# Windowed attention with a max-out layer on one core: weight sums in the third feed-forward bank, fillers in the transpositions' bank, weights loaded behind a group's second part

## The chip, the core and the metric

The kernel runs on one core of one Trainium2 chip. A core has TensorE (PE in the profile, with its weight loads as PEld), VectorE (DVE), ScalarE (ACT), GpSimd (POOL) and SyncE (SP, which here only issues transfers). Each takes its instructions in the order in which they stand in its own queue, and waits at the head of that queue for what an instruction needs. The metric is device time in microseconds, the median of several runs.

## The reference

Attention over 8 batches, 8 heads, 576 positions and 64 values a head, in a window of 128 positions with a bias that falls with distance; then a layer that takes the largest of three products, and one more product:

```python
scores = scale * np.matmul(q, k.transpose(0, 1, 3, 2))
bias = slopes[:, None, None] * (-np.abs(rel).astype(np.float32))[None, :, :]
mask = (rel >= 0) & (rel < window)
scores = np.where(mask, scores + bias[None], -1000000000.0)
attn = np.exp(scores - np.max(scores, axis=-1, keepdims=True))
attn = attn / (np.sum(attn, axis=-1, keepdims=True) + 1e-09)
attn_out = np.matmul(attn, v)
x = attn_out.transpose(0, 2, 1, 3).reshape(B * S, H * D)      # 4608 x 512
h = np.maximum(np.maximum(x @ w1, x @ w2), x @ w3)            # 4608 x 768
out = h @ w_out                                               # 4608 x 512
```

## The kernel before

**Attention.** A task is one batch and one pair of heads: 8 batches make 32 tasks, four to a batch. A task has five steps, one for each block of 128 query rows (the last has 64). For a step, `products` makes the scores on PE (into ps_s, or into ps_m0 and ps_m1), `score` folds the window and adds the bias on DVE (L323, L326, L338), `exps` takes exponentials on ACT (L352), `sums_of` and `normalise` divide by their sums (L360, L361, L373 on ACT or L368 on POOL), `turn` transposes two steps at a time on PE into the bank pt (L382) and ACT copies them out (L386, L392, L395), POOL cuts them to the window (L396, L400), and `mix` multiplies by v on PE into ps_x (L422). After a task's last step ACT copies the mixed values to SBUF (L431).

**Feed-forward.** A batch's x is split in seven combinations of its quarters (`factors_x`, L448 and L449, after DVE differences at L452), each in a high and a low part. A `unit` is one of seven products (L573) of a group; there are eleven groups a batch, nine for the three first matrices and two for the last.

**Weights.** The matrices come as 12 groups of 1 MB. For each, `preparing` takes six steps: `exponents` and `convert` repack the raw words (L144, L145, or L147, L148; then L154 or L158, and L161), and four calls of `part`. Parts 0 and 1 cut the raw words in high and low (`hi_lo`: L167 on ACT, L168 on DVE). Parts 2 and 3 add and subtract them on PE by products with an identity (`plus`) and its negative (`minus`): L178, into a tile of PSUM, which `hi_lo` empties. After part 3 the group is stored (keep, L205) for the later batches. The raw words of a group live in one of two buffers, hs2; `fetch` (L130) loads them through SP's queue. They are last read in part 1.

**Fillers.** `spin` issues products of zeros by zeros on PE (L263) that nobody reads, seven at the start and two at each of 24 steps, into one tile in the bank ps_m2. That bank is the third of the three that the units take in turn (ps_m0, ps_m1, ps_m2), and no unit uses it in the prologue. The transpositions and the weight sums share the bank pt. All these tiles have one buffer each: whoever takes the bank next waits until the one before is read.

**Order.** The prologue is the first batch's attention, with weight steps between (1.3 for each attention step from step 3 on); there is no feed-forward work yet except the first units. From then on a batch's feed-forward runs beside the next batch's attention. Calls are listed with a due time (`at`) and sorted; in the first two batches a scheduler then orders the instructions of each engine by its own estimate, taking the listed order as priority, so that the final queues differ from the code's order. `fix` ends that for PE.

The names in the rows below end in a buffer's number: the same number is the same tile.

Of the kernel before, what the change touches and what calls it, by code (L numbers as in the profile page):

```python
# [8 lines left out]
F32 = mybir.dt.float32  # L9
# [11 lines left out]
LAG_T, LAG_X = 4, 6  # L21
# [1 line left out]
SHIFT = (0, 2, 4)  # L23
O_PACE = 0.285
RING = 2
SPIN, FIRST_SPIN = 2, 7


FEW = 4
# [3 lines left out]
def attention_maxout_kernel(  # L33
# [12 lines left out]
    P = 128  # L46
# [4 lines left out]
    NG = w_all.shape[0]  # L51
    W = 2 * P
# [17 lines left out]
    ps_m = ctx.enter_context(tc.tile_pool(name="ps_m", bufs=1, space=PSUM))  # L70
    ps_s = ctx.enter_context(tc.tile_pool(name="ps_s", bufs=1, space=PSUM))
    ps_t = ctx.enter_context(tc.tile_pool(name="ps_t", bufs=1, space=PSUM))
# [27 lines left out]
    def slopes(hp):  # L100
        for h in (2 * hp, 2 * hp + 1):
            nc.scalar.activation(bias[:, h, :], dist, AF.Copy, scale=-8.0 * 2.0 ** (-8.0 * (h + 1) / H))
        nc.gpsimd.affine_select(
            out=bias0[:, 2 * hp:2 * hp + 2], in_=bias[:, 2 * hp:2 * hp + 2], pattern=[[0, 2], [-1, P]],
            compare_op=ALU.is_ge, fill=-NEG, base=0, channel_multiplier=1,
        )
# [21 lines left out]
    def fetch(g):  # L128
        r = raws[g] = hs_p.tile([P, 4 * DM + DM // 2], I32, name="hs2", bufs=2)
        nc.sync.dma_start(r.bitcast(U8)[:, :16 * DM - 3], w_all[g].bitcast(U8)[:, 3:])  # L130
# [7 lines left out]
    def words(g, j):  # L138
        return pieces(g)[0][:, j * DM:(j + 1) * DM].bitcast(F32)

    def exponents(g, few):
        _, t, top, small = pieces(g)
        if few:
            nc.vector.tensor_scalar(out=small, in0=top, scalar1=-56.0, scalar2=56.0, op0=ALU.max, op1=ALU.min)  # L144
            nc.scalar.activation(t.bitcast(F32), top, AF.Copy, scale=2.0 ** 27)  # L145
        else:
            nc.scalar.activation(small, top, AF.Relu, bias=-56.0)  # L147
            nc.scalar.activation(t.bitcast(F32), top, AF.Relu, scale=-2.0 ** 27, bias=-56.0 * 2.0 ** 27)  # L148

    def convert(g, few):  # L150
        u, t, _, small = pieces(g)
        u = u.bitcast(U32)
        if few:
            nc.vector.scalar_tensor_tensor(  # L154
                out=t, in0=small, scalar=-2.0 ** 27, in1=t.bitcast(F32), op0=ALU.mult, op1=ALU.add
            )
        else:
            nc.vector.scalar_tensor_tensor(  # L158
                out=t, in0=small, scalar=2.0 ** 27, in1=t.bitcast(F32), op0=ALU.mult, op1=ALU.subtract
            )  # L160
        nc.vector.scalar_tensor_tensor(  # L161
            out=u, in0=u, scalar=5, in1=t.bitcast(U32), op0=ALU.logical_shift_right, op1=ALU.bitwise_or
        )

    def hi_lo(t, src):
        pick = (lambda a: t[:, :, a]) if len(t.shape) == 4 else (lambda a: t[:, a])
        nc.scalar.copy(out=pick(0), in_=src)  # L167
        nc.vector.tensor_tensor(out=pick(1), in0=src, in1=pick(0).bitcast(F32), op=ALU.subtract)  # L168

    def group(g):  # L170

        if g < 9:
            return lambda a, e, d=1: wts[g, a // 4][:, a - a // 4 * 4:e - a // 4 * 4:d]
        return lambda a, e, d=1: ow[:, a:e:d, g - 9]

    def added(t, *terms):
        for n, (sign, x) in enumerate([(sign, x[:, a]) for sign, x in terms for a in (1, 0)]):
            nc.tensor.matmul(  # L178
                t, lhsT=sign, rhs=x, start=n == 0, stop=n == 2 * len(terms) - 1, skip_group_check=True,
            )  # L180

    def part(g, n):
        if g < 9 and n == 0:
            place(g, 0)
        if g < 9 and n == 1:
            place(g, 1)
        f = group(g)
        one = lambda k: f(k, k + 1)[:, 0]
        if n < 2:
            src = words(g, n).rearrange("p (k n) -> p k n", k=2)  # L190
            hi_lo(f(0, 2) if n == 0 else f(4, 7, 2), src)
            return
        ps = ps_t.tile([P, 2, W], F32, name="pt")
        if n == 2:
            added(ps[:, 0], (plus, one(1)), (plus, one(6)))
            added(ps[:, 1], (plus, one(0)), (minus, one(1)))
            hi_lo(one(1), ps[:, 0])
            hi_lo(one(5), ps[:, 1])
        else:
            added(ps[:, 0], (plus, one(1)), (minus, one(0)))  # L200
            added(ps[:, 1], (plus, one(4)), (minus, one(1)), (plus, one(0)))
            hi_lo(f(2, 4), ps)
            if g < 9:
                for a in range(2):
                    nc.sync.dma_start(keep[g][a], wts[g, a].bitcast(F32))  # L205

    def place(n, a):
        wts[n, a] = wt_p.tile([P, 4 - a, 2, W], F32R, name=f"wt{a}")

    def ahead(n, a):  # L210

        return n < RING or (n - RING, 6 if a else 3) in used


    g_order = [0, 1, 9, 10, 11, 2, 3, 4, 5, 6, 7, 8]

    def preparing():
        for n, g in enumerate(g_order):
            exponents(g, n < FEW)
            yield  # L220
            convert(g, n < FEW)
            yield
            for k in range(4):
                while g < 9 and not ahead(g, k > 0):
                    yield True
                part(g, k)
                yield
            if n + 2 < NG:
                fetch(g_order[n + 2])

    prepared, owed = 0, 0
    steps_of_weights = preparing()

    def weights(n=0, upto=0):
# [21 lines left out]

    idle = hs_p.tile([P, P + 512], mybir.dt.bfloat16, name="hs")
    nc.vector.memset(idle, 0.0)
    spun = ps_m.tile([P, 512], F32, name="ps_m2")

    def spin(n):
        for _ in range(n):
            tc.keep_in_program_order(nc.tensor.matmul(  # L263
                spun, lhsT=idle[:, :P], rhs=idle[:, P:], start=True, stop=True, skip_group_check=True,
            ))

    fixed = False

    def pe(ins):
        if fixed:  # L270
# [7 lines left out]
    def load(t):  # L278
        b, hp = tasks[t]
        qkt[t] = qk_p.tile([P, 2, S], F32, name="qk")  # L280
        for cs in (slice(0, 2 * P), slice(2 * P, S)) if t == 0 else (slice(0, S),):
            nc.sync.dma_start(qkt[t][:, :, cs], qk[b, hp, :, :, cs])

    def load_v(t):
        b, hp = tasks[t]
        vt[t] = v_p.tile([P, NB, P], F32, name="v")
        nc.sync.dma_start(vt[t], v[b, hp])
# [152 lines left out]
    def later(when, what, *args):  # L440
        todo.append((when, what, args))
        todo.sort(key=lambda x: x[0])
# [3 lines left out]
    def split(out, src, e):  # L446
        hi, lo = out
        nc.scalar.copy(out=hi, in_=src)  # L448
        e.tensor_tensor(out=lo, in0=src, in1=hi.bitcast(F32), op=ALU.subtract)  # L449

    def sub(out, x, y):
        nc.vector.tensor_tensor(out=out, in0=x, in1=y, op=ALU.subtract)  # L452

    def factors_x(b, when, step):
        t0, t1 = [xk[b, k][:, :, :C] for k in range(2)], [xk[b, k][:, :, C:] for k in range(2)]
        b00, b01, b10, b11 = t0[0], t1[0], t0[1], t1[1]
        new = {}

        def tmp():
            new["t"] = xk_p.tile([P, 2, C], F32, name="xt")  # L460
            return new["t"]

        def cut(k, src):
            xs[b, k] = x = xs_p.tile([P, 2, 2, C], F32R, name="xs")
            split((x[:, 0], x[:, 1]), src(), nc.vector)

        t = lambda: new["t"]
        for n, (k, diff, src) in enumerate((
            (0, None, lambda: b00),
            (1, lambda: sub(tmp(), b01, b00), t),  # L470
            (2, lambda: sub(t(), b11, t()), t),
            (3, lambda: sub(b01, b11, b01), lambda: b11),
            (4, None, lambda: b10),
            (5, None, lambda: b01),
            (6, lambda: sub(b10, b10, t()), lambda: b10),
        )):
            if diff:
                later(when + n * step, diff)
            later(when + n * step, cut, k, src)
# [111 lines left out]
    def at(when, what, *args):  # L591
        events.append((when, len(events), what, args))

    n_steps = NP * NB
    shift = [SHIFT[min(b, 2)] for b in range(B)]
    for t, (b, hp) in enumerate(tasks):
        for i in range(NB):
            s = t * NB + i + shift[b]
# [32 lines left out]
            when += pace if u < 77 * b + 63 else O_PACE  # L631
    for u in range(77 * B, 77 * B + 3):
        at(when, unit, u)
    for s in range(3, n_steps + LAG_X):
        at(s + 0.2, weights, 1.3)
    for s in range(n_steps + LAG_X - 2):
        at(s + 0.45, spin, SPIN)

    def fix():
# [2 lines left out]

    at(2 * n_steps + LAG_X + shift[2], fix)
    spin(FIRST_SPIN)
    load(0)
    nc.sync.dma_start(ident, c_ident)
    nc.scalar.copy(out=plus, in_=ident)
    nc.scalar.activation(minus, ident, AF.Copy, scale=-1.0)
    slopes(0)
    fetch(0)  # L650
    load_v(0)
    load(1)
    fetch(1)
    for _, _, what, args in sorted(events, key=lambda e: e[:2]):
# [39 lines left out]
```

## Time and profile before

| what | value |
|---|---|
| median of 3 runs | 819.0 us (817.31 to 820.26) |
| profiled execution | 814.65 us, span 812.9 us |
| mean granted TensorE clock | 0.993 |
| TensorE, VectorE, ScalarE, GpSimd busy | 783.2, 551.0, 536.1, 192.7 us |
| fillers (L263) | 55 products, from 2.5 to 77.2 us |
| first and fourth copy of mixed values (L431) | 36.17 and 79.45 us |
| loads of raw weights (L130) | 12, issued from 2.8 to 142.8 us, median 5.5 us to landing |

A row of a timeline has the start, the length, the engine, the line, the operation, the tile written and those read, their shapes, how many instructions are merged, and in brackets how long the engine stood idle before and what ended that. A matmul of 32-bit numbers can show as two records. A list of waits names who waited for whom: total, times and the longest. The clock is a share of full speed.

### The profile page before, as it was taken

Reading aid. Unit: us, or ns where it says so; the run is one execution under the profiler, and the core shown is the slowest. Engines: PE = TensorE matmul, PEld = TensorE weight load, DVE = VectorE, ACT = ScalarE, POOL = GpSimd, SP = SyncE. Lnnn points to the kernel's source line nnn. Section 1 sums busy time; section 2 is a strip of 40 time slices with the busy share of each in tenths; the row PEclk is TensorE's granted clock in tenths of the full one; section 3 lists DMA queues with packets and bytes.
Section 4 is the critical chain, followed back from the end, with each engine's and each line's share of the span. In section 5 each row is a group of like instructions: output and inputs, shape, how many; then the busy total and the mean of one; then the engine's idle time right before and its main releaser. Section 6 shows DMA issues by size and latency. Waiting matters only on the chain.

```text
span 812.9 us, 18197 instructions
## 1 busy us (share of the span) xinstructions
PE 783.2 (96%) x6543; PEld 687.8 (85%) x6543; DVE 551.0 (68%) x1771; ACT 536.1 (66%) x1796; POOL 192.7 (24%) x412
## 2 busy tenths in 40 slices
PE   7887999999999999999999999999999999999997
PEld 2445877789898999899988998899898989899897
DVE  4776888977577937776567846785667847673662
ACT  5688788677676866676667756775667757652342
POOL 2332213212232212231232212321222213211100
PEclk8999999999999999999999999999999999999999
DMA  6663368585788648873698558873797557765851
GB/s 230 235 225 133 122 247 307 189 288 188 237 276 278 239 134 287 299 257 139 212 313 275 199 173 284 302 258 113 243 318 248 192 199 252 258 214 176 291 204 59
DMA packets 41674, 184.81 MB, mean 227 GB/s; under 512 B 4592, under 2 KB 13552, under 8 KB 32368
## 3 DMA queue, kind: packets, MB, share of 16 engines
q0 software_dynamic: 18144, 115.61, 42.4%
q1 hardware_dynamic: 23296, 67.97, 23.3%
q8 instruction: 52, 0.85, 0.4%
q14 instruction: 38, 0.31, 0.1%
q10 hardware_dynamic: 144, 0.07, 0.0%
HBM read 157.68 MB, written 25.95 MB: 226 GB/s over the span
## 4 chain that ended last, share of the span: by engine, by line
PE 76%; issue 7%; DVE 6%; ACT 5%; DMA 4%; POOL 1%; SPq 0%; POOLq 0%; ACTq 0%; DVEq 0%
PE ps_m L573 54%; PE ps_x L422 8%; PE ps_s L308 6%; PE pt L382 5%; DMA hs<-in_w_all 3%; PE pt L178 2%; ACT p L352 1%; DVE hs L449 1%; DMA wt<-keep 1%; POOL wt L254 1%; DVE s L338 1%; ACT hs L147 1%; DVE t L536 1%; DVE hq L537 1%; DVE ps_s L326 1%
## 5 line engine op out<-in xcount | busy, mean ns | idle before, releaser
L573 PE MATMUL ps_m<-xs,wt 128*128 128x288 f32 x3024 | 430.9, 298 | 7.3 <-DVE xs L449 2.8
L573 PEld LDWEIGHTS ps_m<-xs,wt 128*128 128x128 f32 x3024 | 407.4, 188 | 15.7 <-DVE hq L531 3.0
L582 ACT COPY t<-ps_m 128x288 f32<-128x288 f32 x264 | 104.2, 395 | 73.9 <-PE ps_m L573 72.8
L573 PE MATMUL ps_m<-hs,ow 128*128 128x288 f32 x1008 | 140.5, 296 | 1.2 <-DVE hs L449 0.7
L573 PEld LDWEIGHTS ps_m<-hs,ow 128*128 128x128 f32 x1008 | 134.4, 188 | 3.3 <-DVE hs L449 2.3
L396 POOL TENSOR_SCALAR_AFFINE_SELECT pp<-pr 128x256 f32<-128x256 f32 (+1 forms) x128 | 60.3, 471 | 322.7 <-ACT pr L395 189.7
L352 ACT ACTIVATE p<-s,st 128x128 f32<-128x128 f32 (+1 forms) x320 | 127.4, 402 | 8.5 <-PE pt L382 3.3
L254 POOL DMA_DIRECT2D wt<-keep x126 | 67.8, 538 | 207.3 <-PE ps_m L573 199.4
L373 ACT ACTIVATE p<-p,st 128x128 f32<-128x128 f32 x280 | 97.4, 397 | 17.8 <-DVE st L361 17.8
L536 DVE TENSOR_TENSOR t<-ps_m,t 128x288 f32<-128x288 f32 x144 | 64.5, 452 | 47.3 <-PE ps_m L573 30.4
L338 DVE CUSTOM_DVE_ANT_0 s<-ps_s,bias 128x128 f32<-128x128 f32 (+1 forms) x300 | 76.9, 283 | 18.5 <-PE ps_s L308 13.9
L326 DVE COPY_PREDICATED ps_s<-prev,ps_s 128x256 f32<-128x256 uint8 x120 | 50.8, 423 | 48.4 <-PE ps_s L308 46.6
L422 PE MATMUL ps_x<-pp,v 128*64 128x256 f32 (+3 forms) x768 | 79.9, 322 | 0.6 <-POOL pp L396 0.5
L308 PE MATMUL ps_s<-qk 64*64 64x192 f32 (+1 forms) x1080 | 70.5, 328 | 3.2 <-DVE st L338 3.2
L537 DVE TENSOR_TENSOR hq<-t,hq 128x288 f32<-128x288 f32 x144 | 66.6, 466 | 2.4
L422 PEld LDWEIGHTS ps_x<-pp,v 128*64 128x64 f32 (+1 forms) x768 | 45.8, 136 | 26.5 <-issue 10.7
L395 ACT COPY pr<-pt 128x256 f32<-128x256 f32 x64 | 18.9, 321 | 71.0 <-PE pt L382 71.0
L382 PE MATMUL pt<-ident,p 128*128 128x128 f32 (+1 forms) x320 | 56.9, 286 | 7.9 <-DVE wt L168 3.6
L382 PEld LDWEIGHTS pt<-ident,p 128*128 128x128 f32 (+1 forms) x320 | 33.8, 141 | 34.6 <-issue 18.5
L352 ACT ACTIVATION_READ_ACCUMULATOR p<-s,st 128x1 f32 (+1 forms) x320 | 62.0, 194 | 0.0
L308 PEld LDWEIGHTS ps_s<-qk 64*64 64x64 f32 x1080 | 40.8, 134 | 21.8 <-issue 8.8
L400 POOL TENSOR_SCALAR_AFFINE_SELECT pp<-pr 128x256 f32<-128x256 f32 (+1 forms) x128 | 56.5, 441 | 0.0
(71 smaller groups left out, 760.4 us busy)
## 6 DMA issues: line engine op xcount, KB each, us to landing
wt<-keep POOLq DMA_DIRECT2D x63, 1024.0 KB, 7.5
wt<-keep POOLq DMA_DIRECT2D x63, 768.0 KB, 4.9
qk<-in_qk SPq DMA_DIRECT2D x31, 576.0 KB, 5.8
hs<-in_w_all SPq DMA_DIRECT2D x12, 1023.6 KB, 5.5
v<-in_v SPq DMA_DIRECT2D x32, 320.0 KB, 5.8
keep<-wt SPq DMA_DIRECT2D x9, 1024.0 KB, 5.5
outT<-t SPq DMA_DIRECT2D x64, 144.0 KB, 1.8
keep<-wt SPq DMA_DIRECT2D x9, 768.0 KB, 3.7
```

The source lines that it names most:

```text
L254: nc.gpsimd.dma_start(wts[n, a], keep[n % 9][a])
L308: pe(nc.tensor.matmul(ps[j][d:d + D, o:o + k1 - k0], lhsT=qkt[t][j * D:(j + 1) * D, 0, q0:q0 + D], rhs=qkt[t][j * D:(j + 1) * D, 1, k0:k1] ...
L338: nc.vector.tensor_tensor_reduce(out=s[:n], in0=ps[j][:n, P:2 * P], in1=(bias if i else bias0)[:n, 2 * hp + j, :], scale=-0.125, scalar=3. ...
L352: nc.scalar.activation(p[:n, j], s[:n], AF.Exp, bias=st[:n, 0, a, j:j + 1], scale=-1.0, accum_out=st[:n, 1, a, j:j + 1])
L373: nc.scalar.activation(p[:n, j], p[:n, j], AF.Copy, scale=st[:n, 2, a, j:j + 1])
L382: pe(nc.tensor.transpose(out=pt[:, a, j, :n], in_=p[:n, j], identity=ident[:n, :n]))
L396: nc.gpsimd.affine_select(out=pp[t, i - 1][:, :, 1, :n], in_=r[:, a, :, :n], pattern=[[0, 2], [-1, n]], compare_op=ALU.is_gt, fill=0.0, ba ...
L422: pe(nc.tensor.matmul(x[j * D:(j + 1) * D, c:c + e - a], lhsT=vv[:n, i, j * D:(j + 1) * D], rhs=w[:n, j].rearrange("p a b -> p (a b)")[:, ...
L536: nc.vector.tensor_tensor(out=s, in0=ps, in1=e, op=ALU.add)
L537: nc.vector.tensor_tensor(out=h, in0=s, in1=h, op=ALU.max)
L573: pe(nc.tensor.matmul(ps, lhsT=lt, rhs=rt, start=i == 0 and k in (0, 1, 4), stop=i == len(pairs) - 1, skip_group_check=True,))
L582: nc.scalar.copy(out=e, in_=ps)
```

## The change

Six edits, all in what the prologue does:

- The tile of parts 2 and 3 (L193) is in the bank ps_m2 as long as the first batch's x has not been cut (`begun`), and in pt afterwards.
- `spin` takes a new tile in pt at each call, where it had one in ps_m2.
- Fillers come four at every second step, where they were two at each.
- A group's successor but one is fetched after its part 1, where it was after its part 3.
- Weight steps begin at step 5 with 1.5 for each attention step, where they began at 3 with 1.3.
- At the start the first v is loaded ahead of the identity, and the first bias is made ahead of `plus` and `minus`.

```diff
-SPIN, FIRST_SPIN = 2, 7
+SPIN, FIRST_SPIN = 4, 7
...
-        ps = ps_t.tile([P, 2, W], F32, name="pt")
+        ps = ps_t.tile([P, 2, W], F32, name="pt") if begun else ps_m.tile([P, 2, W], F32, name="ps_m2")
...
                 part(g, k)
+                if k == 1 and n + 2 < NG:
+                    fetch(g_order[n + 2])
                 yield
-            if n + 2 < NG:
-                fetch(g_order[n + 2])
...
-    spun = ps_m.tile([P, 512], F32, name="ps_m2")
 
     def spin(n):
+        spun = ps_t.tile([P, 512], F32, name="pt")
         for _ in range(n):
...
-    fixed = False
+    fixed = begun = False
...
     def factors_x(b, when, step):
+        nonlocal begun
+        begun = True
...
-    for s in range(3, n_steps + LAG_X):
-        at(s + 0.2, weights, 1.3)
-    for s in range(n_steps + LAG_X - 2):
+    for s in range(5, n_steps + LAG_X):
+        at(s + 0.2, weights, 1.5)
+    for s in range(1, n_steps + LAG_X - 2, 2):
         at(s + 0.45, spin, SPIN)
...
     load(0)
+    load_v(0)
     nc.sync.dma_start(ident, c_ident)
+    slopes(0)
+    fetch(0)
     nc.scalar.copy(out=plus, in_=ident)
     nc.scalar.activation(minus, ident, AF.Copy, scale=-1.0)
-    slopes(0)
-    fetch(0)
-    load_v(0)
```

What the scheduler makes of it is seen in the queues. First DVE at the start of the program. Before, the instruction behind the three memsets is the first on the raw weights (hs2_160), ahead of the first scores (s_177 and s_179 are the two heads of step 0):

```order
L258 MEMSET hs_139 128x320
L144 TENSOR_SCALAR hs2_160<-hs2_160 128x1024
L338 ISA s_177,st_176<-ps_s_105,bias0_117 128x128
L338 ISA st_176 128x1
L338 ISA s_179,st_176<-ps_s_105,bias0_117 128x128
```

Now, from the second head of step 0 on:

```order
L338 ISA s_179,st_176<-ps_s_105,bias0_117 128x128
L338 ISA st_176 128x1
L323 COPY_PREDICATED ps_m0_199<-prev_113,ps_m0_199 128x128
L326 COPY_PREDICATED ps_s_105<-prev_113,ps_s_105 128x2x128
L323 COPY_PREDICATED ps_m1_200<-prev_113,ps_m1_200 128x128
L338 ISA s_187,st_176<-ps_s_105,bias_116 128x128
L338 ISA st_176 128x1
L338 ISA s_189,st_176<-ps_s_105,bias_116 128x128
L338 ISA st_176 128x1
L338 ISA s_212,st_211<-ps_m0_199,bias_116 128x128
L338 ISA st_211 128x1
L144 TENSOR_SCALAR hs2_160<-hs2_160 128x1024
```

Five scores stand ahead of L144.

Second, DVE at the last step of the second task (s_427 and s_429 are its two heads). Before, with the second group's raw words hs2_166 and the third's hs2_409:

```order
L338 ISA s_427,st_426<-ps_s_105,bias_116 64x128
L338 ISA st_426 64x1
L154 SCALAR_TENSOR_TENSOR hs2_166<-hs2_166 128x1024
L168 TENSOR_TENSOR wt1_328<-pt_331,wt1_328 128x256
L161 SCALAR_TENSOR_TENSOR hs2_166<-hs2_166 128x1024
L144 TENSOR_SCALAR hs2_409<-hs2_409 128x1024
L168 TENSOR_TENSOR wt0_435<-hs2_166,wt0_435 128x2x256
L168 TENSOR_TENSOR wt0_288<-pt_358,wt0_288 128x2x256
L168 TENSOR_TENSOR wt1_486<-hs2_166,wt1_486 128x2x256
L154 SCALAR_TENSOR_TENSOR hs2_409<-hs2_409 128x1024
L338 ISA s_429,st_426<-ps_s_105,bias_116 64x128
```

Now (s_480 and s_482 are the next task's first step):

```order
L154 SCALAR_TENSOR_TENSOR hs2_166<-hs2_166 128x1024
L168 TENSOR_TENSOR wt0_328<-ps_m2_387,wt0_328 128x256
L338 ISA s_427,st_426<-ps_s_105,bias_116 64x128
L338 ISA st_426 64x1
L338 ISA s_429,st_426<-ps_s_105,bias_116 64x128
L338 ISA st_426 64x1
L338 ISA s_480,st_479<-ps_m0_456,bias0_117 128x128
L338 ISA st_479 128x1
L168 TENSOR_TENSOR wt1_343<-ps_m2_387,wt1_343 128x256
L361 RECIPROCAL st_336<-st_336 128x4
L338 ISA s_482,st_479<-ps_m1_457,bias0_117 128x128
```

The weight operations have moved from between the two heads to both sides of them.

Third, PE at part 3 of the first group. Before, the sums, the fillers and the next transpositions:

```order
L178 MATMUL pt_358<-wt1_328,plus_111 128x256 x2
L178 MATMUL pt_358<-wt0_288,minus_112 128x256 x2
L178 MATMUL pt_358<-wt0_288,plus_111 128x256 x2
L263 LDWEIGHTS hs_139
L263 MATMUL ps_m2_141<-hs_139 128x512
L263 LDWEIGHTS hs_139
L263 MATMUL ps_m2_141<-hs_139 128x512
L382 MATMUL pt_392<-ident_110,p_273 128x64 x2
```

Now:

```order
L178 MATMUL ps_m2_400<-wt1_343,plus_111 128x256 x2
L178 MATMUL ps_m2_400<-wt0_328,minus_112 128x256 x2
L178 MATMUL ps_m2_400<-wt0_328,plus_111 128x256 x2
L263 LDWEIGHTS hs_139
L263 MATMUL pt_438<-hs_139 128x512
L263 LDWEIGHTS hs_139
L263 MATMUL pt_438<-hs_139 128x512
L263 LDWEIGHTS hs_139
L263 MATMUL pt_438<-hs_139 128x512
L263 LDWEIGHTS hs_139
L263 MATMUL pt_438<-hs_139 128x512
L308 MATMUL ps_s_105<-qk_184 64x192 x2
```

The sums and the fillers have changed banks; the transpositions that follow (into pt_466) share theirs with the fillers alone. From some 80 us on the queues hold the same kinds of instructions in nearly the same order in both kernels, and in the last three quarters the same order.

## The prediction

> **What bounds it now.** I read the page first, then a table by stage, the waits of the first stage, and the engines' timelines there. The page has the span and the clock that TensorE was granted, in 40 slices of 20.3 us (tenths of full speed):
>
> ```profile
> span 812.9 us, 18197 instructions
> PEclk8999999999999999999999999999999999999999
> ```
>
> Only the first slice is below 9, so the clock matters at the start if anywhere. The table by stage (length, then busy time and count of PE, PEld, DVE, ACT, POOL, then clock, DMA share, GB/s):
>
> ```profile
> 0.00:83.00 83.00, 64.37 (x472) 35.29 (x472) 55.62 (x186) 61.96 (x204) 23.36 (x53) 0.94 0.59 206
> 83.00:150.00 67.00, 64.67 (x514) 55.36 (x515) 57.91 (x159) 52.50 (x152) 18.94 (x29) 1.00 0.63 231
> 150.00:800.00 650.00, 645.35 (x5497) 588.83 (x5497) 436.10 (x1425) 419.60 (x1437) 150.39 (x330) 1.00 0.69 233
> ```
>
> From 83 us on TensorE is the bound: 64.67 of 67, then 645.35 of 650. Before it none is: PE lacks 18.6 us, ACT 21.0, DVE 27.4. That stage is the prologue, and its end is read from the chain:
>
> ```profile
> 79.54 0.53 ACT xk L431
> ...
> 82.96 3.33 PE ps_m L573 x23
> ```
>
> The fourth copy of mixed values (L431, task 3) lets the x factors be cut, and with them PE runs full. The change can pay by bringing this L431 forward; the same PE work follows it, bar six score products. In front of it ACT waited (from the list of waits of the first 83 us: total, times, longest):
>
> ```profile
> ACT pr L386 <- PE pt L382: 3.1, 2, 2.8
> ACT p L352 <- PE pt L382: 3.0, 3, 1.7
> ACT hs L145 <- DVE hs L144: 2.3, 1, 2.3
> ACT wt L167 <- DVE hs L161: 2.1, 1, 2.1
> ACT hs L147 <- DMA hs<-in_w_all: 1.7, 1, 1.7
> ACT p L352 <- issue: 1.4, 1, 1.4
> ```
>
> **The change, part by part.** *The start.* From the timelines of DVE, ACT and PE (start, length, engine, line, operation; in brackets the idle time before it), and a five-microsecond stage:
>
> ```profile
> 8.93 0.69 DVE L144 TENSOR_SCALAR hs<-hs 128x1024 int8<-128x1024 int8 x1 [6.53 <-DMA hs<-in_w_all]
> 6.44 0.30 ACT L647 CAST plus<-ident 128x128 fp32r<-128x128 f32 x1 [2.51 <-DMA ident<-in_ident]
> 10.67 0.41 ACT L352 ACTIVATE p<-s,st 128x128 f32<-128x128 f32 x1
> 6.83 1.04 PE L263 MATMUL ps_m<-hs 128*128 128x512 bf16 x4
> 16.22 1.91 PE L263 MATMUL ps_m<-hs 128*128 128x512 bf16 x4
> 11.56 0.76 PE L308 MATMUL ps_s<-qk 64*64 64x192 f32 x12 [1.70 <-DVE st L338]
> 5.00:10.00 5.00, 4.86 (x42) 1.86 (x40) 1.07 (x6) 1.25 (x5) 0.41 (x1) 1.00 1.00 400
> ```
>
> The first score products are done when the fillers (L263) begin at 6.83, yet the scoring instruction L338 stands behind L144, which waits for the first weights and ends at 9.6. Now five score pieces stand ahead of L144, and L145 behind their exponentials. The identity comes behind v (320 KB, about 0.8 us at the 400 GB/s of that stage), so its casts end near 7.8 and the first exponential starts there, not at 10.67: up to 2.8 us. I take 2.3, the L145 wait; 1.5 if the identity lands a microsecond late.
>
> *The clock.* One-microsecond stages of PE (busy, clock, DMA):
>
> ```profile
> 12.00:13.00 1.00, 0.32 (x8) 1.00 0.12 49
> 13.00:14.00 1.00, 0.00 (x0) 0.81 0.87 217
> 14.00:15.00 1.00, 0.92 (x4) 0.50 0.97 391
> 20.00:21.00 1.00, 1.00 (x7) 0.78 0.06 16
> 34.00:35.00 1.00, 1.00 (x4) 0.55 1.06 451
> ```
>
> PE stood nearly idle from 10 to 14; then the clock was half until about 20.2, four fillers taking 1.91 us for 1.04. That is 6.2 us at half, 3.1 lost, and ACT's wait of 2.8 for transpositions stands behind it. With scores 2.5 us earlier, the second scores, the first transpositions and three products of the next task fill about half of that gap. I take 2.5 (the clock mostly holds); bounds 0 and 3.1. The second, shorter drop at 34 I leave as it is. The Trainium skill ("TensorE: Matmul & The Clock Gate", Part 1) says the gate drops to 4/8 after an idle window of about 3.4 us and lifts after a busy one; the 0.50 agrees, while no single gap here was that long. By that rule alone the shorter gaps would keep the clock, and the term would be 3.1.
>
> *Weights behind attention.* Weight steps begin at step 5, 1.5 a step, not at 3 with 1.3. The knot they made on DVE:
>
> ```profile
> 27.68 0.28 DVE L338 CUSTOM_DVE_ANT_0 s<-ps_s,bias 64x128 f32<-64x128 f32 x1
> 34.80 0.27 DVE L338 CUSTOM_DVE_ANT_0 s<-ps_s,bias 64x128 f32<-64x128 f32 x1
> ```
>
> Seven microseconds pass between two halves of one step's scores, eight weight operations between them, by the order of instructions. In the new order the halves are neighbours, and each large weight operation has scores on both sides. ACT's 2.1 for L161 goes; bounds 0 and 2.1, as the same operations still have to be done before 83 us. By the order of the new program, it puts less ACT work ahead of the fourth L431: four exponentials (0.41 as at 10.67), a normalising pair and one L147 fewer:
>
> ```profile
> 74.38 0.70 ACT L373 ACTIVATE p<-p,st 128x128 f32<-128x128 f32 x2
> 78.43 1.11 ACT L147 ACTIVATE hs<-hs 128x1024 int8<-128x1024 int8 x1
> ```
>
> That is 3.4 us moved into 83 to 150, where the stage's row leaves ACT 14.5 us and DVE 9.1. Six score products move too, 0.7 us of PE (the row at 11.56 is six, two records each). I take 2.0, as not all of it will fall into free time; bounds 0 and 2.7.
>
> *The banks.* PE's timeline has three transpositions behind weight sums in the one bank pt, and one wait of a sum for its own predecessor:
>
> ```profile
> 29.50 0.50 PE L178 MATMUL pt<-wt,plus 128*128 128x256 f32 x2 [1.03 <-DVE wt L168]
> 33.20 0.70 PE L382 MATMUL pt<-ident,p 64*128 64x64 f32 x4 [1.81 <-DVE wt L168]
> 44.13 0.70 PE L382 MATMUL pt<-ident,p 128*128 128x128 f32 x4 [1.32 <-DVE wt L168]
> 75.92 0.70 PE L382 MATMUL pt<-ident,p 128*128 128x128 f32 x4 [1.90 <-DVE ow L168]
> ```
>
> With the sums in ps_m2 the last three go, 5.03 us of PE; the first stays, ps_m2 having one buffer too. On ACT they show as 3.0 (exponentials whose p buffer is held until it is turned) and part of the 1.4. I take 3.0; bounds 0 and 4.4.
>
> *Fillers in pt.* As many as before (55), in fours after the first seven, but ten of the twelve fours now need pt, filled by transpositions, to be copied out by ACT. What that takes:
>
> ```profile
> 49.79 0.66 PE L382 MATMUL pt<-ident,p 128*128 128x128 f32 x4
> 50.08 1.18 ACT L147 ACTIVATE hs<-hs 128x1024 int8<-128x1024 int8 x1 [1.74 <-DMA hs<-in_w_all]
> 51.90 0.41 ACT L395 COPY pr<-pt 128x256 f32<-128x256 f32 x1
> 54.04 0.44 PE L382 MATMUL pt<-ident,p 128*128 128x128 f32 x2
> 54.57 0.59 ACT L386 COPY pr<-pt 128x512 f32<-128x512 f32 x1
> ```
>
> From the last transposition to a free bank 0.7 us in the second case, 1.9 where L147 lies between; ten times their mean is 13 us. But in the new order most fours have five or more products between transposition and filler. Four have little cover, at some 0.5: I take 2.0 lost; bounds 0 and 13. Behind a waiting filler on PE stand products whose operands POOL makes from the same copy, so part of that wait is not new.
>
> *Fetches.* SP's queue shows that loading already stood ahead of the stores:
>
> ```profile
> 24.79 0.33 SPq L130 DMA_DIRECT2D hs<-in_w_all x1
> 29.47 4.04 SPq L205 DMA_DIRECT2D keep<-wt x2
> ```
>
> It is held by the buffer, not by its place, so the move itself is worth 0. The 1.7 of L147 for its weights (fetch 43.77, landed 50.05) comes through the compute order; group 11 is now asked for after group 9's second part and used later on ACT. I take 1.0; bounds 0 and 1.7.
>
> Sum: 2.3 + 2.5 + 2.1 + 2.0 + 3.0 + 1.0 − 2.0 = 10.9 us. Span 812.9 − 10.9 = 802.0; the profiled execution (814.65, 1.75 around the span) would be 803.8. It lies 4.35 below the median of 819.0, so for the median I say 808.1. All upper ends together give 2.8 + 3.1 + 2.1 + 2.7 + 4.4 + 1.7 = 16.8, thus 802.2; the lower ones give 1.5 and −13, thus 830.5.
>
> **Rivals.** *Slower: fillers hold PE.* If ACT copies pt out late at every filler, as at 51.90 (1.9 us), and nothing lies between, ten waits cost 19 us. It decides when the mean wait passes the other six terms, 12.9 over 10, so 1.3 us each. At 1.9 it gives 819.0 + 19 − 12.9 = 825. For it: ACT's long weight operations of 1.1 us stand among the copies. Against it: the 0.7 of the copy at 54.57, and the products that the new order puts between.
> *The clock swings.* Fillers that wait, and in pairs of steps, leave more gaps. Two more drops like 14 to 20.2 (3.1 each) and none saved: 10.9 − 2.5 − 6.2 = 2.2, thus 816.8. The Trainium skill's same page ("A second HAM failure mode: psum-queue depth-cycling") speaks for this: cycling banks, PE idles briefly between groups and the gate swings. The page's clock row speaks against it: from the second slice on it reads 9, though PE idled 1.32 us at 44.13 and 1.90 at 75.92.
> *Given back behind 83 us.* With the prologue shorter, weights for groups 2 to 8 are asked for sooner, on a DVE that is 86% busy (57.91 of 67). If the moved work's term and half of the rest stall PE there, 10.9 − 2.0 − 4.5 = 4.4 remains: 814.6.
> *Nothing.* The knots return elsewhere, as ACT (62 of 83) and DVE have no other order that suits both: 819.
>
> **How the numbers follow.** Forecast 0.52; given back 0.20; clock 0.13; nothing 0.08; slower 0.07. About 0.3% (2.5 us) can be told from no change, so below 816.5 is faster: the first two and half of the clock's case, 0.79; same 0.14; slower 0.07. The likeliest case has 802 to 813. The range reaches into the clock's case: 802 to 817, with a tenth or so outside on each side.
>
> **What would show it.** First exponential near 8 us. Clock full from 14 to 20. No transposition waiting for L168 before the fourth L431, which comes near 68 to 70. L263 with idle of at most 0.5 each. PE in the 67 us after it as full as before. It is wrong if L263 carries microseconds of idle behind ACT's copies, if the clock row has more halves, or if PE waits for weights after the prologue.

## The result, and the profile after

The changed kernel takes 808.95 us (median of 4 runs, 808.59 to 809.97), the kernel before beside it 819.63 (4 runs, 817.31 to 824.83): a ratio of 0.9863, 95% interval 0.9815 to 0.9911. The profiled execution took 808.59 us. The page after, first the span, then PE's busy time and its clock by slices:

```profile
span 806.9 us, 18196 instructions
...
PE   8997999999999999999999999999999999999987
...
PEclk9999999999999999999999999999999999999999
```

The first slice of the clock is at 9 now. The table by stage, columns as in the prediction:

```profile
0.00:83.00 83.00, 70.65 (x515) 41.29 (x516) 62.05 (x200) 66.61 (x213) 29.02 (x54) 0.96 0.56 203
83.00:150.00 67.00, 64.71 (x519) 53.90 (x519) 57.18 (x162) 53.55 (x158) 17.85 (x29) 1.00 0.68 252
150.00:800.00 650.00, 644.41 (x5497) 590.23 (x5496) 430.55 (x1409) 415.19 (x1425) 150.24 (x329) 1.00 0.69 232
```

PE is busy for 6.3 us more in the first 83 us and as long as before in the next 67 (64.71, it was 64.67). All that is gained is gained in the prologue. ACT's timeline there, the first exponential and three copies of mixed values (first, third, fourth task):

```profile
7.30 0.40 ACT L352 ACTIVATE p<-s,st 128x128 f32<-128x128 f32 x1 [0.38 <-DVE st L338]
...
26.04 0.63 ACT L431 COPY xk<-ps_x 128x576 f32<-128x576 f32 x1
...
55.80 0.64 ACT L431 COPY xk<-ps_x 128x576 f32<-128x576 f32 x1
...
68.41 0.64 ACT L431 COPY xk<-ps_x 128x576 f32<-128x576 f32 x1
```

The exponential stood at 10.67, the four copies at 36.17, 51.12, 65.50 and 79.45 (now 26.04, 38.97, 55.80, 68.41). So 10.1 us are won in the first task alone and 11.0 by the fourth. PE's timeline shows what becomes of them. The first row is the start of the long run of products on the x factors, at 82.96 before:

```profile
72.45 3.46 PE L575 MATMUL ps_m<-xs,wt 128*128 128x288 f32 x24 [2.29 <-DVE xs L449]
78.14 0.74 PE L178 MATMUL pt<-ow,plus 128*128 128x256 f32 x2 [2.24 <-DVE ow L168]
110.94 0.51 PE L178 MATMUL pt<-wt,plus 128*128 128x256 f32 x2 [0.46 <-ACT pr L386]
```

PE starts 10.5 us earlier. Then it waits 2.24 us for one weight difference, since on ACT two long weight operations stand ahead of two casts: L167, which the difference L168 needs, and L448 (at 76.25), which L449 needs, the operation ahead of it on DVE:

```profile
74.03 1.14 ACT L147 ACTIVATE hs<-hs 128x1024 int8<-128x1024 int8 x1
75.19 1.21 ACT L148 ACTIVATE hs<-hs 128x1024 f32<-128x1024 int8 x1
76.81 0.41 ACT L167 CAST ow<-pt 128x256 fp32r<-128x256 f32 x1
```

Behind that gap the clock is at half, as PE's one-microsecond stages show (busy, clock, DMA share, GB/s; the first four rows are an earlier stretch of half clock):

```profile
12.00:13.00 1.00, 0.76 (x8) 1.00 0.87 270
13.00:14.00 1.00, 1.00 (x12) 0.69 0.99 376
14.00:15.00 1.00, 1.00 (x9) 0.50 0.80 310
...
16.00:17.00 1.00, 1.00 (x4) 0.61 0.03 8
...
78.00:79.00 1.00, 0.86 (x4) 0.61 0.00 0
79.00:80.00 1.00, 1.00 (x7) 0.50 0.00 0
...
81.00:82.00 1.00, 1.00 (x14) 0.68 0.00 0
```

The weight sum at 110.94 stood at 117.88 in the trace before:

```profile
117.88 0.50 PE L178 MATMUL pt<-wt,plus 128*128 128x256 f32 x2 [0.73 <-ACT pr L386]
```

So 6.9 of the 10.5 us are left there. The span ends 6.0 ahead. PE's waits for stored weights (wt<-keep), 1.3 us before and 2.5 now, are enough for the last 0.9.

The profiled executions thus differ by 6.1 us (814.65 to 808.59), the medians by 10.7. Most of what lies between can be put down to the clock. I call (1 − mean granted clock) × time the lost clock of a run. Over the 58 runs of the kernel before that stood beside all the kernels below (813.3 to 826.6 us, median 818.7) it is 9.4 us on average, and the time follows it: 0.72 us for each us lost, correlation 0.93, and 812.2 us where none is lost. The profiled execution of before lost 5.1, so it was one of its quicker ones. The changed kernel's four runs lost 3.8 on average and lie within 1.4 us. If each us of lost clock is worth the same 0.72 us in the changed kernel, (9.4 − 3.8) × 0.72 = 4.0 us of the gain is clock, and the other 6 or so are stalls. That split is an estimate; no run shows the two apart.

### The profile page after: what moved, and what is told of

The parts are those of the page before. It is cut to its first block, busy times and chain, and to the rows that moved or that the text cites. A ratio compares the mean times of both kernels' runs of the same rounds, so it can differ in the third digit from the quotient of the medians.

```text
span 806.9 us, 18196 instructions
## 1 busy us (share of the span) xinstructions
PE 782.5 (97%) x6543; PEld 687.7 (85%) x6543; DVE 550.7 (68%) x1771; ACT 535.7 (66%) x1796; POOL 197.1 (24%) x412
## 4 chain that ended last, share of the span: by engine, by line
PE 78%; issue 8%; DVE 7%; ACT 3%; DMA 2%; POOL 2%; POOLq 0%; ACTq 0%; DVEq 0%
PE ps_m L575 54%; PE ps_x L422 8%; PE ps_s L308 7%; PE pt L382 5%; PE pt L178 2%; DMA wt<-keep 1%; PE pt L263 1%; DVE hs L449 1%; PE ps_m L178 1%; POOL wt L254 1%; DVE s L338 1%; DMA hs<-in_w_all 1%; DVE ps_s L326 1%; PE ps_m L308 1%; DVE t L538 1%
## 5 line engine op out<-in xcount | busy, mean ns | idle before, releaser
L308 PEld LDWEIGHTS ps_s<-qk 64*64 64x64 f32 x1080 | 41.1, 134 | 20.6 <-issue 10.2
L382 PE MATMUL pt<-ident,p 128*128 128x128 f32 (+1 forms) x320 | 55.0, 281 | 1.2 <-POOL p L368 1.0
```

Source lines behind the costliest of these rows:

```text
L308: pe(nc.tensor.matmul(ps[j][d:d + D, o:o + k1 - k0], lhsT=qkt[t][j * D:(j + 1) * D, 0, q0:q0 + D], rhs=qkt[t][j * D:(j + 1) * D, 1, k0:k1] ...
L382: pe(nc.tensor.transpose(out=pt[:, a, j, :n], in_=p[:n, j], identity=ident[:n, :n]))
```

## The experiments

Twelve kernels: each edit undone in the changed kernel, three edits made alone, and four on the fillers. "Fourth copy" is the fourth L431 in that kernel's profile, "lost" the mean lost clock over its runs. The ratio is to the kernel before on the same chip. In banks_alone the lines behind the edit have numbers lower by one, in banks_undone higher by one. The kernels did not all run on one chip: the sets of the kernel before that ran beside them have medians of 818.2, 822.1 and 818.2 us. So times of two kernels that differ by less than some 4 us are told apart by their ratios, if at all. Against the changed kernel's ratio (0.9815 to 0.9911), the intervals of start undone, weights undone, fetch undone, fillers in ps_m2, no fillers and longer fillers overlap; the others lie above it, banks alone at its edge.

| kernel | median us (range, runs) | ratio, 95% interval | lost us | first, fourth copy |
|---|---|---|---|---|
| before | 818.7 (813.3 to 826.6, 58) | 1 | 9.4 | 36.17, 79.45 |
| changed | 809.0 (808.6 to 810.0, 4) | 0.9863 (0.9815 to 0.9911) | 3.8 | 26.04, 68.41 |
| start alone | 814.0 (812.1 to 816.4, 7) | 0.9954 (0.9928 to 0.9980) | 6.2 | 33.21, 77.10 |
| weights alone | 818.0 (813.6 to 823.8, 10) | 1.0005 (0.9967 to 1.0042) | 7.1 | 28.58, 78.53 |
| banks alone | 817.3 (812.8 to 819.6, 10) | 0.9945 (0.9911 to 0.9980) | 7.8 | 37.27, 79.68 |
| banks undone | 817.2 (812.9 to 820.6, 10) | 0.9989 (0.9960 to 1.0018) | 8.8 | 25.10, 78.00 |
| start undone | 812.2 (809.4 to 813.2, 4) | 0.9891 (0.9820 to 0.9962) | 4.7 | 30.92, 72.44 |
| weights undone | 810.4 (808.7 to 813.1, 4) | 0.9881 (0.9820 to 0.9942) | 5.9 | 36.53, 73.68 |
| fetch undone | 808.6 (806.1 to 811.4, 4) | 0.9886 (0.9850 to 0.9922) | 4.2 | 25.32, 67.63 |
| pace undone | 814.5 (812.5 to 818.2, 10) | 0.9946 (0.9913 to 0.9980) | 4.8 | 28.95, 75.78 |
| fillers in ps_m2 | 808.3 (805.5 to 810.0, 4) | 0.9849 (0.9788 to 0.9910) | 3.0 | 25.21, 65.09 |
| no fillers | 806.9 (806.0 to 807.4, 4) | 0.9848 (0.9802 to 0.9894) | 9.5 | 29.45, 62.81 |
| double fillers | 815.4 (810.7 to 816.6, 10) | 0.9951 (0.9921 to 0.9980) | 3.2 | 28.54, 76.15 |
| longer fillers | 807.3 (806.6 to 808.1, 6) | 0.9853 (0.9812 to 0.9894) | 2.3 | 26.49, 66.32 |

Over the 14 rows the time goes with the fourth copy: 0.70 us for each us that it comes earlier, correlation 0.96. The end of the prologue is where the change pays, as the prediction had it. How it pays is another matter. A copy's time is that of one execution: in the changed kernel and fetch_undone PE, DVE, ACT and POOL have the same instructions in the same order up to 84 us, yet the fourth copy comes at 68.41 and 67.63. The first has a stretch of half clock at 13 us, the second has none there. And start_alone's profile is of one of its slowest runs (816.35), with 10.2 us lost where its mean is 6.2.

**start_alone.** Before, with the edit at the start alone.

```diff
     load(0)
+    load_v(0)
     nc.sync.dma_start(ident, c_ident)
+    slopes(0)
+    fetch(0)
     nc.scalar.copy(out=plus, in_=ident)
...
-    slopes(0)
-    fetch(0)
-    load_v(0)
```

> The kernel before with one edit: at the start v ahead of the identity, bias ahead of plus and minus. In its order of instructions DVE's first weight operation (L144) now stands behind five scores, as in the changed kernel, while the knot of weight operations between the two halves of a score in the second task stays. Theory 'two knots' (the 10 us that the first copy of mixed values, L431, came forward are two separate knots on DVE, one for each of two edits): first exponential near 7.3 us instead of 10.7, first L431 2.5 to 4 us earlier than 36.17, time 815 to 817. Rival 'banks' (the gain is from weight sums and transpositions no longer sharing a bank): first L431 near 36, time 818 to 820. Rival 'any edit reshuffles' (the scheduler makes another order of every edit, and the time follows that, not the edit): anywhere from 810 to 822.

Measured 814.0, 4.2 us less than before (818.2 on that chip). By the intervals this edit and banks_alone both pay by themselves; against all 58 runs of before (818.7) they bring 4.7 and 1.5 us.

**weights_alone.** Before, with weight steps from step 5, 1.5 for each.

```diff
-    for s in range(3, n_steps + LAG_X):
-        at(s + 0.2, weights, 1.3)
+    for s in range(5, n_steps + LAG_X):
+        at(s + 0.2, weights, 1.5)
```

> The kernel before with one edit: weight steps from step 5 with 1.5 for each attention step, not from 3 with 1.3. In its order the knot in the second task is gone (the two halves of the score are neighbours), while L144 still heads DVE's queue at the start. 'Two knots': first exponential near 10.7 as before, first L431 5 to 8 us earlier than 36.17, time 812 to 815. 'Banks': transpositions still wait for weight sums in pt (some 5 us of PE in the prologue), first L431 near 34 to 36, time 817 to 820. 'Any edit reshuffles': anywhere from 810 to 822.

Measured 818.0: no difference. Yet its first copy comes at 28.58, 7.6 us ahead of before, and its fourth at 78.53, 0.9 ahead. The 7.6 us are given back within the prologue. PE's timeline shows where:

```profile
61.95 0.62 PE L382 MATMUL pt<-ident,p 128*128 128x128 f32 x2 [0.46 <-ACT p L373]
63.80 0.97 PE L178 MATMUL pt<-ow,plus 128*128 128x256 f32 x6 [1.23 <-ACT pr L386]
66.56 0.65 PE L422 MATMUL ps_x<-pp,v 128*64 128x256 f32 x4 [0.97 <-POOL pp L396]
73.07 1.06 PE L382 MATMUL pt<-ident,p 128*128 128x128 f32 x4 [2.34 <-DVE ow L168]
83.53 1.81 PE L573 MATMUL ps_m<-xs,wt 128*128 128x288 f32 x6 [3.09 <-DVE xs L449]
```

In the fourth task sums and transpositions take turns in the one bank pt: a sum waits 1.23 us until ACT has copied a transposition out, a transposition waits 2.34 until DVE has read a sum.

**banks_alone.** Before, with sums in ps_m2 and fillers in pt (two at each step).

```diff
-        ps = ps_t.tile([P, 2, W], F32, name="pt")
+        ps = ps_t.tile([P, 2, W], F32, name="pt") if begun else ps_m.tile([P, 2, W], F32, name="ps_m2")
...
-    spun = ps_m.tile([P, 512], F32, name="ps_m2")
...
+        spun = ps_t.tile([P, 512], F32, name="pt")
...
```

> The kernel before with one edit: weight sums of the prologue in ps_m2, fillers in pt, still two at each step. After the first four runs: undoing the banks took the whole gain (817.2), while the first copy of mixed values still came at 25; the copies after it came late, and TensorE's clock was halved three times between 61 and 90 us. Theory 'banks keep the clock' (a transposition that waits for a weight sum leaves PE idle, the clock falls to half for 3.4 or 6.8 us, and at half clock PE is the bound of the last tasks): alone it is worth less than in company, as the knots on DVE at the start stay; mean granted clock 0.993 or more, 811 to 815. Rival 'only together' (each edit alone is given back at the next bound): 816 to 819. Rival 'reshuffle' (no edit has a price of its own): anywhere.

Measured 817.3 beside 822.1 of before on that chip: 0.9 to 0.2% faster by the interval, though 822.1 is the highest of the medians of before. The fourth copy in its profile is where it was (79.68).

**banks_undone.** The changed kernel with the sums in pt, and the fillers in one ps_m2 tile.

```diff
-        ps = ps_t.tile([P, 2, W], F32, name="pt") if begun else ps_m.tile([P, 2, W], F32, name="ps_m2")
+        ps = ps_t.tile([P, 2, W], F32, name="pt")
...
+    spun = ps_m.tile([P, 512], F32, name="ps_m2")
...
-        spun = ps_t.tile([P, 512], F32, name="pt")
```

> The changed kernel with the banks as before: weight sums in pt with the transpositions, fillers in one tile of ps_m2. Both knots stay gone in its order. 'Two knots': first L431 near 26 to 28 as in the changed kernel (26.04), PE waits for L168 at transpositions come back (3 to 5 us) but no filler waits for a copy, so 809 to 812. 'Banks': first L431 near 34, time 816 to 819. My prediction's two terms for it were 3.0 gained and 2.0 lost, so 810.

Measured 817.2: nearly the whole gain is gone, though all other edits are in. The first task is as quick as in the changed kernel (25.10), the fourth copy comes at 78.00. PE's timeline has the same waits as weights_alone, to the hundredth:

```profile
61.07 0.99 PE L178 MATMUL pt<-ow,plus 128*128 128x256 f32 x6 [1.23 <-ACT pr L387]
...
72.54 1.06 PE L383 MATMUL pt<-ident,p 128*128 128x128 f32 x4 [2.34 <-DVE ow L168]
83.11 5.89 PE L576 MATMUL ps_m<-xs,wt 128*128 128x288 f32 x23 [3.09 <-DVE xs L450]
```

Line numbers are one higher in this kernel. The 23 products at 83.11 took 5.89 us, where 24 took 3.46 in the changed kernel: the clock is at half (its one-microsecond stages):

```profile
62.00:63.00 1.00, 1.00 (x7) 0.50 0.00 0
67.00:68.00 1.00, 1.00 (x6) 0.50 0.47 156
73.00:74.00 1.00, 1.00 (x5) 0.50 0.00 0
77.00:78.00 1.00, 1.00 (x13) 0.50 0.07 16
83.00:84.00 1.00, 0.89 (x4) 0.50 0.05 18
88.00:89.00 1.00, 1.00 (x6) 0.50 0.00 0
```

So the denser weight steps need the banks: with them the fourth task is a place where sums and transpositions follow each other closely. The reverse doesn't hold: weights_undone, below, has the banks without these steps and takes 810.4. No kernel here has these two edits alone together. The order of instructions isn't the changed kernel's either (by the traces it differs from 13.7 us on for PE and from 14.9 us on for DVE). fillers_in_ps_m2, below, differs from the same places on and keeps the gain, which speaks for the bank; how much of the 8.2 us is the waits and how much the order isn't shown.

**start_undone.**

```diff
-    load_v(0)
     nc.sync.dma_start(ident, c_ident)
-    slopes(0)
-    fetch(0)
...
+    slopes(0)
+    fetch(0)
+    load_v(0)
```

> The changed kernel with the start as before: L144 heads DVE's queue again and the first exponential comes near 10.5. Alone this edit brought 4.2 us (814.0). 'Banks keep the clock': most of the three microseconds at the start come back: 811 to 813, first L431 near 29. 'Only together' says more than that, 814 or later. If the later tasks are the bound whatever the start does: 809.

Measured 812.2: 3.2 us more than the changed kernel, where the edit by itself brought 4.2. The intervals of the two ratios overlap.

**weights_undone.** Steps from 3, 1.3 for each, again.

```diff
-    for s in range(5, n_steps + LAG_X):
-        at(s + 0.2, weights, 1.5)
+    for s in range(3, n_steps + LAG_X):
+        at(s + 0.2, weights, 1.3)
```

> The changed kernel with weight steps from step 3 at 1.3 again. In its order the knot in the second task is back: nine rows of DVE between the two halves of a score, and L144 of the third group, which waits for its load, among them. Alone the edit brought nothing (818.0). 'Banks keep the clock': the knot costs 3 to 5 us of the first task, and the weights are earlier for the last tasks, which gives 1 or 2 back: 810 to 813, first L431 near 30. If the time follows the banks alone: 808 to 810.

Measured 810.4: 1.4 us, and the intervals of the two ratios overlap. In the profiles the fourth copy comes 5.3 us later than in the changed kernel and the end 2.9 (811.44 against 808.59), with 6.8 us of clock lost there, not 3.4. Where the rest is given back isn't shown.

**fetch_undone.** A group's successor but one is fetched after part 3 again.

```diff
-                if k == 1 and n + 2 < NG:
-                    fetch(g_order[n + 2])
                 yield
+            if n + 2 < NG:
+                fetch(g_order[n + 2])
```

> The changed kernel with the fetch of a group's successor but one behind part 3 again. In its order of SP's queue the loads stand in nearly the same places between the stores. 'Two knots' and 'banks' and my prediction (the move itself is worth 0): 808 to 810, first L431 at 26, fourth at 68 to 69. Rival 'fetch' (weights come sooner and that frees the later tasks): fourth L431 1 to 3 us later, time 811 to 812.

Measured 808.6: nothing, as the prediction had it.

**pace_undone.** Fillers two at every step, in pt.

```diff
-SPIN, FIRST_SPIN = 4, 7
+SPIN, FIRST_SPIN = 2, 7
...
-    for s in range(1, n_steps + LAG_X - 2, 2):
+    for s in range(n_steps + LAG_X - 2):
```

> The changed kernel with one edit undone: fillers come two at every step again, not four at every second, in pt as in the changed kernel. Fillers-cost theory (what the prediction took 2.0 us off for): a filler's price is its wait for a free pt; twice as many places of half the length ask for pt twice as often, so up to 2 us worse, 810 to 811. Rival (fillers fall into time in which PE had nothing to do, and no filler showed idle of its own in the changed kernel): no difference, 808 to 810, with the clock lost as in the changed kernel, some 3 to 5 us.

Measured 814.5: 5.5 us, more than either reason gave. The price isn't idle time of the fillers. PE's timeline in the fourth task (no row of L263 there shows idle):

```profile
63.72 0.65 PE L422 MATMUL ps_x<-pp,v 128*64 128x256 f32 x4 [1.73 <-POOL pp L396]
65.42 0.65 PE L422 MATMUL ps_x<-pp,v 128*64 128x256 f32 x2 [1.05 <-POOL pp L396]
...
68.16 0.65 PE L263 MATMUL pt<-hs 128*128 128x512 bf16 x1
69.16 0.85 PE L422 MATMUL ps_x<-pp,v 128*64 128x256 f32 x2 [0.36 <-issue]
```

and ACT's:

```profile
61.01 1.14 ACT L148 ACTIVATE hs<-hs 128x1024 f32<-128x1024 int8 x1
62.04 0.57 ACT L386 COPY pr<-pt 128x512 f32<-128x512 f32 x1
...
68.39 0.59 ACT L167 CAST ow<-ps_m 128x512 fp32r<-128x512 f32 x1 [2.45 <-PE ps_m L178]
...
72.21 0.54 ACT L395 COPY pr<-pt 128x256 f32<-128x256 f32 x2 [2.12 <-PE pt L382]
```

A weight operation stands ahead of the copy out of pt, POOL cuts late, PE waits for it at the head of its queue with the weight sums behind, and ACT waits for those: another order that the scheduler made from another list. In the changed kernel the same product waits 0.62 us. That twice as many claims on pt lead the scheduler to this order is a guess; only the order and the time are shown.

**fillers_in_ps_m2.** The changed kernel, with a new ps_m2 tile for each four.

```diff
-        spun = ps_t.tile([P, 512], F32, name="pt")
+        spun = ps_m.tile([P, 512], F32, name="ps_m2")
```

> The changed kernel, but fillers in new tiles of ps_m2, with the weight sums; pt is the transpositions' alone. 'Banks keep the clock': transpositions wait for no sum, as in the changed kernel; a filler now waits for DVE's L168 of the last sum where it waited for ACT's copy, so fillers come later in the sums' stretches: 807 to 811, clock 0.993 or more. If fillers in pt, just behind the transpositions, are what holds the clock: clock 0.990 or less and 813 or more.

Measured 808.3, the same as the changed kernel. What counts is that the sums are out of pt; the fillers may stand with either.

**no_fillers.** The 48 fillers after the first seven are left out.

```diff
-SPIN, FIRST_SPIN = 4, 7
+SPIN, FIRST_SPIN = 0, 7
```

> The changed kernel with the first seven fillers only; the 48 later products of zeros (0.24 us each at full clock, 11.5 us of PE) are left out. Clock theory: without them PE is emptier in the prologue, the clock is half in more pieces, and each us of clock lost costs 0.7 us, as over the runs of the kernel before. Lost clock rises from 3.8 to some 8 to 12 us, so 812 to 815, with a wider spread. Rival (fillers hold PE in order, the 2.0 us that the prediction took off for them, and are worth nothing): 806 to 807. If PE is not what ends the prologue at all, neither: 808 to 810 with more clock lost.

Measured 806.9, the lowest of all: below every run of the changed kernel, though on another chip and with ratios whose intervals overlap. Both theories are half right. The clock does suffer (9.5 us lost, as much as before the change), as the first stage's row shows:

```profile
0.00:83.00 83.00, 64.69 (x493) 42.73 (x494) 63.90 (x205) 68.51 (x222) 29.14 (x56) 0.90 0.59 209
```

Clock 0.90, not 0.96. But PE is busy for 6.0 us less in it, ACT and DVE for 1.9 us more each, and the fourth copy comes 5.6 us earlier. At 0.72 us each the 5.7 us of clock cost 4.1, so by an estimate from these two kernels the fillers, or the order that the scheduler makes around them, hold the rest of the program by some 6 us.

**double_fillers.** Eight at every second step.

```diff
-SPIN, FIRST_SPIN = 4, 7
+SPIN, FIRST_SPIN = 8, 7
```

> The changed kernel with eight fillers at every second step in place of four: 48 more, 11.5 us of PE at full clock. PE lacks 12.4 us of the first 83 in the changed kernel. Fillers-hold-PE theory: they fit only in part into that, and what stands behind them comes late, so 2 to 6 us slower, 811 to 815. Clock theory: the clock stays full (lost below 2 us, where it was 3.8), which is worth 1.5 us, and most of the fillers fall into idle time: 807 to 809, and the runs agree within 1 us.

Measured 815.4, with 3.2 us lost. More fillers hardly save clock and hold everything else: the fourth copy moves to 76.15.

**longer_fillers.** Fillers in ps_m2, and two more fours after the first products on x factors.

```diff
-        spun = ps_t.tile([P, 512], F32, name="pt")
+        spun = ps_m.tile([P, 512], F32, name="ps_m2")
...
-    for s in range(1, n_steps + LAG_X - 2, 2):
+    for s in range(1, n_steps + LAG_X + 2, 2):
```

> The changed kernel with fillers in new ps_m2 tiles (808.3 us, no different from pt) and two more fours, which by the order of instructions stand behind the first products of the x factors, where PE idles and the clock falls to half from 78.4 to 81.7 us in the changed kernel (1.7 us lost). Clock theory: that piece goes, 1.2 us of it to be seen in the time: 806.5 to 807.5, a candidate for the fastest. Rival (the wait of 2.2 us for the difference L168 stays what it is, and the products in front of it have time): 808 to 809.

Measured 807.3 (lost 2.3 us). That is 1.0 below the same kernel without the two fours (fillers_in_ps_m2, 805.5 to 810.0), with overlapping ranges. Each of its six runs is below the four of the changed kernel, by 1.6 us in the medians, but on another chip, and the intervals of the ratios overlap. In its profile the half clock behind the long run of products is gone and only a stretch at 13 to 16 is left, where fillers_in_ps_m2 has one at 75 to 79 and none at 13. PE's wait for the difference is shorter with the fours (1.11 us, not 2.18), but it ends as long behind the fourth copy (9.4 us) in both. So here the fillers stand where PE has nothing else to do; that they pay isn't shown by the runs.

## Why the prediction was right, and where it was not

The forecast of 808.1 and the 808.95 measured agree better than the working deserves.

*From the profile to the median.* This step failed. The sum of 10.9 us was made against the profiled execution, which was to come to 803.8 and took 808.59: it gained 6.1. The prediction then carried the profiled execution's 4.35 us below the median over as if it were a constant. It is lost clock, which the change itself makes smaller and steadier: the changed kernel's profiled execution lies 0.4 us below its median. The two errors, 4.8 and 4.0 us, cancel.

*Start: 2.3.* Right in kind, too small. The first exponential came 3.4 us earlier, not 2.8 at most, and waits for scores, not for the identity. The edit brought 4.2 by itself; the 3.2 by which the changed kernel is slower without it isn't clear of the spread.

*Clock: 2.5.* The size was of the right order, 4.0 over the runs by the estimate above, the place was not. The clock isn't full from 14 to 20: it is at half from 13.4 to 16.8, where the prediction had counted 6.2 us. PE is busier ahead of it than before (0.76 from 12 to 13, where it had 0.32, then full), and that wasn't enough. Nor does the order of instructions decide it. In fetch_undone, with the same order, PE stood idle for longer (1.33 us) and kept its clock there:

```profile
12.00:13.00 1.00, 0.00 (x0) 1.00 0.94 234
13.00:14.00 1.00, 0.89 (x8) 1.00 0.67 184
```

So whether this stretch is lost differs between executions, and a term that counts on it is partly luck. The Trainium skill ("TensorE: Matmul & The Clock Gate", "HAM oscillation — how this bites in real kernels") gives as the rule no PE gaps over some 3.4 us. No run here supports that as a safe bound: the gap ahead of the drop at 78 is 2.24 us, ahead of the one at 13 no single gap is over 1 us (the longest is 0.98), while fetch_undone's 1.33 us cost nothing. What the prediction cited for the rival (many short idle times, a clock that swings) fits better, but no run here shows how much idle time it takes.

*Weights behind attention: 2.1 and 2.0.* Over-sized as a term of its own: 0 alone, 1.4 in the changed kernel, which the ratios don't tell from nothing.

*Banks: 3.0, and fillers in pt: −2.0.* The mechanism was right: no transposition waits for L168 before the fourth L431, which came at 68.41 where 68 to 70 was said. The net of 1.0 was the worst-sized term: undone it costs 8.2 us. It was priced from three waits in the trace of before. Among the waits that it avoids are those of weights_alone and banks_undone (1.23 and 2.34 us in the fourth task), which come with the denser weight steps, and the trace of before can't show them. The −2.0 was wrong: no filler waits for its bank, and in the other bank they cost the same. What fillers cost is rather their time in PE's order, by the estimate above some 6 us, less the 4 that they save in clock.

*Fours at every second step.* Counted as nothing by itself; the other pace is 5.5 us slower, with another order of the queues.

*Fetches: 0 and 1.0.* The move is worth nothing, as said. L147's wait of 1.7 for its weights is no longer in ACT's list of waits of the first 83 us (one of 1.1 comes behind them); its share of the time wasn't measured apart.

*The rival "given back behind 83 us".* It happened in part: 3.6 of the 10.5 us are lost between 72 and 111, not by PE waiting for weights of groups 2 to 8 in its units, but by one wait of a sum for a difference (L168), 2.24 us, and by 3.4 us of half clock behind it, worth up to 1.7. The slower case (fillers that wait for pt and hold PE) didn't occur. Fillers do hold PE otherwise: the other pace costs 5.5 us, twice as many 6.4.

*The sum.* Undone one by one, the edits cost 3.2 + 1.4 + 8.2 − 0.4 + 5.5 = 17.9 us, where together they bring 10.7; the three tried alone bring 4.2, 0.2 and 4.9. (Of these differences only those of banks undone, pace undone, start alone and banks alone are clear of the spread.) A sum of terms, each priced by itself, was the wrong form: each edit changes the list that the scheduler orders, and with it where the next one bites. How much of each price is the edit and how much the order that happened to come of it stays open.

## What to carry to other kernels

Before work is packed closer on an engine that runs in order, separate the chains that share a one-buffer bank: here the packing without the separation brought nothing (818.0 by itself, 817.2 with all other edits), while the separation without the packing kept 810.4. Where a scheduler orders the queues, price edits together, and read each from the end of the stage (here the fourth copy), not from the first place where it shows, and from more than one execution where the clock differs between them. Look at how the time of one kernel spreads with its clock before a gain read from one profiled execution is carried to a median.

## What was not expected of the hardware

The half clock comes in stretches of 3.4 us or two, three or four times that: by the one-microsecond stages each costs 1.7, 3.4, 5.1 (without fillers) or 6.8 us (start_alone from 27.7 us on and banks_alone from 13.0 on), in all 14 profiles up to the last few us. It can follow gaps of 1 or 2 us, and with one and the same order of instructions it comes in one execution and not in another. Over the 58 runs of the unchanged kernel each us of clock lost went with 0.72 us of time, and they spread over 13 us with it (813.3 at a mean clock of 0.997, 826.6 at 0.980). Products of zeros that keep the clock up are not free: without them the kernel lost 5.7 us more clock and still was not slower (806.9); doubled everywhere they cost 6.4 us. Two more fours in a gap took one stretch of half clock out of the profile; their gain of 1.0 us isn't clear of the spread.
